# Sigmoid attention and a bilinear layer on one core: bursts of three with the first product group in whole feature blocks, high parts by ScalarE from the 14th burst, later decoding, the first load of k in two pieces

## The chip, the cores and the metric

The kernel runs on one core of a Trainium2 chip. The metric is device microseconds of one execution; the time before is the median of three runs. Engines are called TensorE (PE in the rows, PEld for its weight loads), VectorE (DVE), ScalarE (ACT), GpSimd (POOL) and SyncE (SP), which only issues transfers here.

## The reference

```python
# q, k, v: (8, 12, 448, 64); tokens 8 * 448 = 3584, d_model 768, d_ff 1024
scores = scale * np.matmul(q, k.transpose(0, 1, 3, 2)) - np.log(S)
attn = 1.0 / (1.0 + np.exp(-scores))
x = np.matmul(attn, v)            # heads side by side: (3584, 768)
a, b = x @ w1, x @ w2             # 768 x 1024 each
h = a * b @ w3                    # 1024 x 1024
out = h @ w_out                   # 1024 x 768
```

The weights come as 64-bit floats, and the kernel decodes them on the chip.

## The kernel before, in words

**Attention.** 96 pairs of batch and head make 48 pairs of heads; two of those pairs form a quad `t`, and a quad has seven items: three chunks of 128 keys for the first pair, one short item that holds the last 64 keys of both pairs, and three chunks for the second pair. 24 quads give 168 items in one list. `sizes` cuts the list into bursts. A burst `k` does, in the order of the program: `prepare` of its items (transfers of later q, k and v; at item (0, 1) and (1, 0) the split of the pair that comes next into a high and a low part, where `hi_cast` says which engine makes the high part and VectorE subtracts the low part); some units of other work; the scores of its items (six matmuls for an ordinary item, eight for a short one) each followed by ScalarE's sigmoid; then the attends (four matmuls, eight for a short one) of the burst before. Finished attends are copied out by ScalarE (`combine`, L334). The output of a sigmoid has four buffers.

**Banks.** Two pairs of banks (`sp`) hold scores, two `av` banks hold attends, and an upper pair of banks holds either `third`, the scores of the third item of a burst, or `up0` and `up1`, the accumulators of products. `share_upper` switches it, and the first write under the new name waits for the last reader under the old one.

**Products.** The first layer is done in four groups `g` of two batches each, by a scheme with seven products for a feature block of 128 (L533). A group is eight feature blocks of 7 x 3 x 3 = 63 matmuls, 504 in all (`GROUP`). `up(g)` yields them one matmul at a time; `take(filler, n)` puts n of them at a place in the program. The partial sums leave by ScalarE copies (products 0 and 2 of a block) and VectorE additions (the others, L500 and L503). Behind each product `beside` takes units of other work.

**Where the products stand.** The first group is spread over a window of bursts, `WINDOW`. Before, the window is bursts 18 to 45 (numbered from 0), all of two items, and behind every second one stand 36 matmuls of products. The next two groups stand whole behind the bursts in `blocks`, 51 and 57, which also have two items. The last group comes after attention.

**Other work.** `change` holds 21 units (`Units`) that split the operands of the next group. `weights` decodes w1 and w2: for each feature block 12 steps on VectorE (six for each of the two weights, with one magnitude by ScalarE for each, L89) and 11 steps that make the seven operands of the block (`divide`: a cast by ScalarE, L79, and a subtraction by VectorE, L80) and four differences. The steps of a block's operands stand between the decoding steps of the next block. That is 1 + 96 + 88 = 185 steps. Before a product whose operand does not yet exist, the missing steps are forced (`next(weights)`). All engines run the instructions in the order of the program (`manual_schedule`).

**After attention** come the last group of the first layer, the product of w3 and w_out, and the second layer. The change does not touch them.

Of the kernel before, what the change touches and what calls it, by code (L numbers as in the profile page):

```python
# [11 lines left out]
F32 = mybir.dt.float32  # L12
# [13 lines left out]
def sigmoid_attention_bilinear_ffn(  # L26
# [16 lines left out]
    nc = tc.nc  # L43
    B, H, D, S = qT.shape
    DM, DF = w1.shape[0], w1.shape[1] // 2
    NT = B * S
    P = 128
# [76 lines left out]
    pa = phase_a.enter_context(tc.tile_pool(name="pa", bufs=2, side="right"))  # L124
# [11 lines left out]
    def load_pair(n, queues=(nc.sync, nc.sync)):  # L136
        b, hp = divmod(n, NPAIR)
        heads = slice(2 * hp, 2 * hp + 2)
        qk = pa.tile([P, 2, S], F32, name="qk", bufs=4)
        for i, src in enumerate((qT, kT)):  # L140
            queues[i].dma_start(out=qk[:, i], in_=src[b, heads].rearrange("h d s -> (h d) s"))
        return qk

    def load_v(t, queue=nc.sync):
# [44 lines left out]
    def scores(high, low, c, third, qk):  # L189

        at = c * P
        sp = score_banks(third)
        terms = ((high, high), (high, low), (low, high)) if high else ((qk, qk),)
        for m, (k, q) in enumerate(terms):
            for j, rows in enumerate(HEADS):
                nc.tensor.matmul(  # L196
                    sp[:, j], k[rows, 1, at:at + P], q[rows, 0],
                    start=m == 0, stop=m == len(terms) - 1,
                )
        return sp  # L200

    def short_scores(two, third):

        sp = score_banks(third)
        for u, qk in enumerate(two):
            for j, rows in enumerate(HEADS):
                nc.tensor.matmul(  # L207
                    sp[HEADS[u], j], qk[rows, 1, FULL:], qk[rows, 0], start=True, stop=True
                )
        return sp  # L210

    def attention(sp):
        a = pa.tile([P, 2, S], F32, name="a", bufs=4)
        sigmoid(a, sp)
        return a
# [18 lines left out]
    KH = NK // 2  # L234
# [111 lines left out]
    def prepare_weights():  # L346

        raw = {}

        def load(j):  # L350
            if j < 2 * NF:
                fc, i = divmod(j, 2)
                raw[j] = load_words(
                    words((w1, w2)[i], slice(fc * P, (fc + 1) * P)), p1, nc.gpsimd, 3
                )

        extras = iter(())
        for j in range(3):
            load(j)
        yield  # L360
        nxt = magnitude(raw[0], p1, 3)
        for fc in range(NF):
            fs = []
            for i in range(2):
                f = nxt
                j = 2 * fc + i
                fs.append(f)
                pops = POPS[i] if fc else (0,) * 6
                for step, _ in enumerate(decode(raw[j], f)):
                    if step == 4 and j + 1 < 2 * NF:  # L370
                        nxt = magnitude(raw[j + 1], p1, 3)
                    if step == 5:
                        del raw[j]
                        load(j + 3)
                    yield
                    for _ in range(pops[step]):
                        yield from one(extras)
            extras = finish_weights(fc, fs)
        for _ in range(sum(sum(pops) for pops in POPS)):
            yield from one(extras)  # L380
# [62 lines left out]
    for ic in range(NF):  # L443
# [3 lines left out]
        for ms in (slice(0, NM), slice(NM, DM)):  # L447
            src = w_out[ic * P:(ic + 1) * P].rearrange("p (m u) -> p m u", u=2)[:, ms]
            jobs.append((src, wo_dram[ic, :, ms]))
    def prepare_rest():  # L450

        raw = {}

        def load(i):
            if i < len(jobs):
                raw[i] = load_words(jobs[i][0], p2[0], nc.sync, 4)

        for i in range(3):
            load(i)
        for _ in range(6):  # L460
            yield
        f = magnitude(raw[0], p2[0], 3)
        for i, (_, dst) in enumerate(jobs):
            load(i + 3)
            for step, _ in enumerate(decode(raw.pop(i), f)):
                if step == 4 and i + 1 < len(jobs):
                    following = magnitude(raw[i + 1], p2[0], 3)
                yield
            nc.gpsimd.dma_start(out=dst, in_=f)
            f = following  # L470
# [96 lines left out]
    def take(stream, n):  # L567
        done = 0
        for _ in itertools.islice(stream, n):
            done += 1  # L570
        return done
# [20 lines left out]
    assert len(quad) == TILES  # L592
    items = [(t, x) for t in range(B * NQ) for x in quad]
    GROUP = NF * 7 * KH * 3
    sizes = [3] * 18 + [2] * 28 + [3] * 5 + [2] + [3] * 5 + [2] + [3] * 8
    WINDOW = (18, 46)
    blocks = {51: 1, 57: 2}
    NBURST = len(sizes)
    starts = [sum(sizes[:k]) for k in range(NBURST + 1)]
    bursts = [items[i:i + n] for i, n in zip(starts, sizes)] + [[]]  # L600
# [3 lines left out]
    def beside(g, n):  # L604

        if g == 0:
            take(change, 1)
            take(weights, 2)
        elif not take(change, 1):
            take(rest, 2)  # L610

    qks, splits, vvs = {}, {}, {}
    qks[0] = load_pair(0, (nc.sync, nc.scalar))
    qks[1] = load_pair(1)
    vvs[0] = load_v(0)
    ready = pm.tile([P, 1], F32, name="ready")
# [2 lines left out]
    weights = prepare_weights()  # L619
    for n in (2, 3):  # L620
        qks[n] = load_pair(n)
    filler = rest = iter(())
    change = Units(0)
# [40 lines left out]
    def short_at(burst, at):  # L664

        shorts = [item for item in burst if item[1] is None]
        rest_of = [item for item in burst if item[1] is not None]
        if len(burst) == 3 and burst[1][1] is None:
            return shorts + rest_of if at == 0 else rest_of + shorts
        return list(burst)  # L670

    def prepare(t, x, hi_cast):

        if x == (0, 1):
            splits[2 * t + 1] = split_pair(qks[2 * t + 1], hi_cast)
        elif x == (0, 2) and t + 1 < B * NQ:
            vvs[t + 1] = load_v(t + 1)
        elif x == (1, 0) and t + 1 < B * NQ:
            splits[2 * t + 2] = split_pair(qks[2 * t + 2], hi_cast)
        elif x == (1, 1) and t + 2 < B * NQ:  # L680
            for n in (2 * t + 4, 2 * t + 5):
                qks[n] = load_pair(n)

    for k in range(NBURST + 1):
        if k == WINDOW[1]:
            phase_1.close()
            px.append(phase_x.enter_context(tc.tile_pool(name="px", bufs=1, side="left")))
            p2.append(phase_2.enter_context(tc.tile_pool(name="p2", bufs=2, side="right")))
            rest = prepare_rest()
        in_window = WINDOW[0] <= k < WINDOW[1]  # L690
        hi_cast = nc.scalar.copy if in_window or k in blocks else nc.vector.tensor_copy
        burst = bursts[k]
        for t, x in burst:
            prepare(t, x, hi_cast)
        if k < WINDOW[0]:
            if k == 1:
                next(weights)
            elif k > 1:
                take(change, 3)
                take(weights, 3 if k < 9 else 2 if k < 13 else 1)  # L700
        elif not in_window and k not in blocks and k < NBURST:
            take(change, 4 if k < 51 else 3)
        now = []
        for i, (t, x) in enumerate(short_at(burst, -1)):
            if x is None:
                sp = short_scores((qks.pop(2 * t), qks.pop(2 * t + 1)), i == 2)
            else:
                u, c = x
                if (k, i) == (0, 0):
                    high = low = None  # L710
                else:
                    high, low = splits[2 * t + u]
                sp = scores(high, low, c, i == 2, qks.get(2 * t + u))
            now.append((t, x, attention(sp)))
        if k == NBURST:
            take(change, 4)
            filler = up(NG - 1)
            take(filler, 9)
        by_place = {item[:2]: item for item in now}
        for item in previous:  # L720
            attend_item(*item)
        previous = [by_place[item] for item in short_at(burst, 0)]
        if k == WINDOW[0]:
            filler = up(0)
        if in_window:
            take(weights, 3 if k > WINDOW[0] + 1 else 0)
            done = k + 1 - WINDOW[0]
            if done % 2 == 0:
                upto, since = (GROUP * i // (WINDOW[1] - WINDOW[0]) for i in (done, done - 2))
                take(filler, upto - since)  # L730
            if k + 1 == WINDOW[1]:
                take(filler, 10)
                change = Units(1)
                take(weights, 10 ** 6)
                for n in range(RING - 1):
                    load_weights(NF * 7 + n)
        elif k in blocks:
            filler = up(blocks[k])
            take(filler, GROUP + 10)
            change = Units(blocks[k] + 1)  # L740
# [280 lines left out]
```

## Time and profile before

| what | us |
|---|---|
| median of three runs | 966.53 (966.41 to 967.92) |
| the profiled execution | 964.66 |
| its span in the profile | 962.9 |
| TensorE busy | 955.6 |
| VectorE busy | 657.1 |
| ScalarE busy | 400.2 |

The span runs from the first to the last instruction of the profiled execution; its time adds what lies around them. Busy times of matmuls are modelled, since matmuls overlap; what one costs is best read as the distance from its start to the next one's. The granted TensorE clock is 1.00, the upper of its two levels, 2.4 GHz, in every stretch of the profile.

### The profile page before, as it was taken

What the parts mean: (1) busy time and instruction counts of PE and PEld (TensorE: products, weight loads), DVE (VectorE), ACT (ScalarE), POOL (GpSimd) and SP (SyncE); (2) the same over time, 40 slices, a digit from 0 to 9 for tenths busy, and PEclk for the clock granted to TensorE, in tenths of its full rate; (3) what the DMA queues carried; (4) which work ended last, traced back from release to release, by engine and by line L of the source; (5) the groups of instructions that cost most, each with busy time, mean ns of one, the idle gap of its engine ahead of it and who ended that gap; (6) DMA issues with size and microseconds to landing.
All of it is one profiled execution on the core that took longest, in us unless ns stands there. A gap on an engine that the chain in (4) does not pass through costs nothing.

```text
span 962.9 us, 14120 instructions
## 1 busy us (share of the span) xinstructions
PE 955.6 (99%) x5236; PEld 756.4 (79%) x5236; DVE 657.1 (68%) x1060; ACT 400.2 (42%) x583; POOL 104.8 (11%) x182
## 2 busy tenths in 40 slices
PE   9999999999999999999999999999999999999998
PEld 5444666676674999957999747999999999999997
DVE  5869778887639788899888628444465657474752
ACT  7887456556548121263221474112243523232230
POOL 1110123222200012110111100211000000000000
PEclk9999999999999999999999999999999999999999
DMA  8864577776645899975999734988431033343402
GB/s 268 254 214 132 190 258 240 244 259 233 234 130 171 293 380 379 381 274 173 366 375 355 240 93 131 355 295 285 165 141 62 29 127 123 115 144 111 157 30 86
DMA packets 93781, 204.37 MB, mean 212 GB/s; under 512 B 9872, under 2 KB 57104, under 8 KB 93712
## 3 DMA queue, kind: packets, MB, share of 16 engines
q1 hardware_dynamic: 78432, 142.40, 44.0%
q0 software_dynamic: 15136, 60.83, 17.6%
q8 instruction: 42, 0.69, 0.3%
q10 hardware_dynamic: 144, 0.23, 0.1%
q14 instruction: 27, 0.22, 0.1%
HBM read 148.37 MB, written 55.05 MB: 211 GB/s over the span
## 4 chain that ended last, share of the span: by engine, by line
PE 95%; DVE 2%; DMA 1%; ACT 1%; issue 1%; SPq 0%; DVEq 0%; ACTq 0%
PE up L533 42%; PE av L220 11%; PE sp L196 8%; PE av L985 7%; PE sp L985 7%; PE up L985 7%; PE av L853 3%; PE sp L853 3%; PE av L228 2%; PE third L196 1%; PE sp L207 1%; DMA vv<-vL 1%; PE third L207 1%; ACT a L177 0%; DVE low L80 0%
## 5 line engine op out<-in xcount | busy, mean ns | idle before, releaser
L533 PE MATMUL up<-hS,w 128*128 128x448 f32 x702 | 214.6, 366 | 0.0
L533 PE MATMUL up<-hA,w 128*128 128x448 f32 x510 | 159.5, 367 | 0.3 <-ACT a L177 0.3
L177 ACT ACTIVATE a<-sp,bias 128x896 f32<-128x896 f32 x132 | 129.9, 1010 | 49.8 <-PE sp L196 24.6
L533 PEld LDWEIGHTS up<-hS,w 128*128 128x128 f32 x702 | 131.8, 188 | 14.7 <-issue 3.5
L533 PE MATMUL up<-lS,w 128*128 128x448 f32 x351 | 128.2, 365 | 0.0
L220 PE MATMUL av<-a,vv 128*64 128x448 f32 x576 | 122.8, 551 | 0.1
L533 PEld LDWEIGHTS up<-hA,w 128*128 128x128 f32 x510 | 95.8, 188 | 13.3 <-issue 4.5
L533 PE MATMUL up<-lA,w 128*128 128x448 f32 x255 | 93.2, 365 | 0.0
L220 PEld LDWEIGHTS av<-a,vv 128*64 128x64 f32 x576 | 35.5, 136 | 67.8 <-issue 67.3
L500 DVE TENSOR_TENSOR u<-up,p 128x448 f32<-128x448 f32 x64 | 39.9, 623 | 55.4 <-PE up L533 52.2
L542 ACT COPY p<-up 128x448 f32<-128x448 f32 x31 | 16.6, 534 | 146.8 <-PE up L533 141.5
L533 PEld LDWEIGHTS up<-lS,w 128*128 128x128 f32 x351 | 65.9, 188 | 5.2
L985 PE MATMUL av<-gh,wo 128*128 128x448 f32 x224 | 68.6, 367 | 0.0
L985 PE MATMUL sp<-gh,wo 128*128 128x448 f32 x224 | 68.6, 367 | 0.0
L985 PE MATMUL up<-gh,wo 128*128 128x448 f32 x224 | 68.5, 367 | 0.0
L500 DVE TENSOR_TENSOR u<-up,u 128x448 f32<-128x448 f32 x64 | 39.8, 622 | 32.4 <-PE up L533 31.8
L79 ACT CAST gh<-gf 128x896 fp32r<-128x896 f32 x40 | 35.7, 944 | 56.2 <-PE sp L985 50.0
L80 DVE TENSOR_TENSOR gl<-gf,gh 128x896 fp32r<-128x896 f32 x40 | 41.9, 1087 | 22.7 <-ACT gh L79 22.7
L80 DVE TENSOR_TENSOR low<-qk,high 128x896 fp32r<-128x896 f32 x47 | 51.3, 1091 | 7.4 <-ACT high L79 6.3
L89 ACT ACTIVATE f<-raw 128x768 f32<-128x768 f32 (+2 forms) x48 | 34.5, 718 | 50.5 <-DMA w_dram<-f 17.0
L196 PEld LDWEIGHTS sp<-high 64*128 64x128 f32 x232 | 21.9, 185 | 42.8 <-ACT a L177 31.0
L548 ACT COPY c<-up 128x448 f32<-128x448 f32 x31 | 16.6, 534 | 85.7 <-PE up L533 60.0
(145 smaller groups left out, 1778.3 us busy)
## 6 DMA issues: line engine op xcount, KB each, us to landing
w<-w_dram SPq DMA_DIRECT2D x168, 384.0 KB, 5.9
gf<-g_dram SPq DMA_DIRECT2D x16, 896.0 KB, 5.7
w_dram<-w POOLq DMA_DIRECT2D x36, 384.0 KB, 4.7
raw<-w POOLq DMA_DIRECT2D x16, 768.0 KB, 6.2
qk<-qT SPq DMA_DIRECT2D x48, 224.0 KB, 4.8
qk<-kT SPq DMA_DIRECT2D x47, 224.0 KB, 4.9
out<-o_sb SPq DMA_DIRECT2D x47, 224.0 KB, 2.0
vv<-vL SPq DMA_DIRECT2D x24, 384.0 KB, 3.5
```

The source lines that it names most:

```text
L79: hi_engine(out=dst_hi, in_=src)
L80: lo_engine.tensor_tensor(out=dst_lo, in0=src, in1=dst_hi, op=ALU.subtract)
L89: nc.scalar.activation(f, raw[..., 1].bitcast(F32), AF.Abs, scale=HW_SCALE)
L177: nc.scalar.activation(dst, src, AF.Sigmoid, bias=bias[:n], scale=scale)
L196: nc.tensor.matmul(sp[:, j], k[rows, 1, at:at + P], q[rows, 0], start=m == 0, stop=m == len(terms) - 1,)
L207: nc.tensor.matmul(sp[HEADS[u], j], qk[rows, 1, FULL:], qk[rows, 0], start=True, stop=True)
L220: nc.tensor.matmul(acc[cols, :S], vv[:, c, at:at + D], a[:, j], start=start, stop=stop,)
L228: nc.tensor.matmul(acc[cols, :S], vs[HEADS[u], cols], a[HEADS[u], j], start=ends[u][0], stop=ends[u][1],)
L500: nc.vector.tensor_tensor(out=out, in0=a, in1=b, op=ALU.add)
L533: nc.tensor.matmul(a, w[:, i, kc], x, start=bool(start) and kc == 0 and m == 0, stop=bool(stop) and kc == KH - 1 and m == 2, skip_group_ch ...
L853: nc.tensor.matmul(acc, a[:, jc], w[:, jc, ms], start=(jc == 0 and m == 0), stop=(jc == NF - 1 and m == 2),)
L985: nc.tensor.matmul(acc, w[:, fc, ms], g[:, fc], start=start and fc == 0 and m == 0, stop=fc == NH - 1 and m == 2, skip_group_check=True,)
```

## The change

The bursts all have three items. The window becomes bursts 18 to 36, and the first group stands there in whole feature blocks of 63 matmuls behind bursts 19, 22, 24, 27, 29, 32, 34 and 36. The two whole groups stand behind bursts 42 and 48, of three items as well. ScalarE makes the high parts from burst 13 to the end of the window, before from burst 18. Decoding steps: three per burst up to burst 10 (before: to 8), two in 11 and 12, none from 13 to 19 (before: one per burst from 13 to 17), four per burst in the window from burst 20 (before: three), two behind a product of the first group, one behind the last two of each block (before: always two). The first pair's k is loaded in two pieces on ScalarE's queue, the first 128 columns first; q stays on SP's.

```diff
+    def load_first_pair():
+        qk = pa.tile([P, 2, S], F32, name="qk", bufs=4)
+        q, k = (src[0, :2].rearrange("h d s -> (h d) s") for src in (qT, kT))
+        nc.scalar.dma_start(out=qk[:, 1, :P], in_=k[:, :P])
+        nc.sync.dma_start(out=qk[:, 0], in_=q)
+        nc.scalar.dma_start(out=qk[:, 1, P:], in_=k[:, P:])
         return qk
...
-    sizes = [3] * 18 + [2] * 28 + [3] * 5 + [2] + [3] * 5 + [2] + [3] * 8
-    WINDOW = (18, 46)
-    blocks = {51: 1, 57: 2}
+    sizes = [3] * 56
+    WINDOW = (18, 37)
+    FIRST_BLOCKS = [WINDOW[0] + i - 1 for i in itertools.accumulate((2, 3, 2, 3, 2, 3, 2, 2))]
+    blocks = {42: 1, 48: 2}
...
         if g == 0:
             take(change, 1)
-            take(weights, 2)
+            take(weights, 2 if n % 7 < 5 else 1)
...
-    qks[0] = load_pair(0, (nc.sync, nc.scalar))
+    qks[0] = load_first_pair()
...
-        hi_cast = nc.scalar.copy if in_window or k in blocks else nc.vector.tensor_copy
+        hi_cast = nc.scalar.copy if 13 <= k < WINDOW[1] or k in blocks else nc.vector.tensor_copy
...
-                take(weights, 3 if k < 9 else 2 if k < 13 else 1)
+                take(weights, 3 if k < 11 else 2 if k < 13 else 0)
         elif not in_window and k not in blocks and k < NBURST:
-            take(change, 4 if k < 51 else 3)
+            take(change, 4 if k < 42 else 3)
...
         if in_window:
-            take(weights, 3 if k > WINDOW[0] + 1 else 0)
-            done = k + 1 - WINDOW[0]
-            if done % 2 == 0:
-                upto, since = (GROUP * i // (WINDOW[1] - WINDOW[0]) for i in (done, done - 2))
-                take(filler, upto - since)
+            take(weights, 4 if k > WINDOW[0] + 1 else 0)
+            if k in FIRST_BLOCKS:
+                take(filler, 7 * KH * 3)
```

## Rows read from the trace of the kernel before

**Rows 1.** From the page: the busy time of each engine with its share of the span and its instructions, and the chain of waits that ended last, by engine.

```profile
PE 955.6 (99%) x5236; PEld 756.4 (79%) x5236; DVE 657.1 (68%) x1060; ACT 400.2 (42%) x583; POOL 104.8 (11%) x182
...
PE 95%; DVE 2%; DMA 1%; ACT 1%; issue 1%; SPq 0%; DVEq 0%; ACTq 0%
```

**Rows 2.** Timeline of TensorE, the early stretch with bursts of three: the first scores of a burst, and those seven bursts later. Columns: start in us, length in us, engine, line, operation, output and inputs, count, in brackets the idle time before it and what ended it.

```profile
45.55 0.47 PE L196 MATMUL sp<-high 64*128 64x448 f32 x2
...
77.98 0.47 PE L196 MATMUL sp<-high 64*128 64x448 f32 x2
```

**Rows 3.** The same view in the window, bursts of two: the start of attention behind products and the start of the next products, three times, then the start of attention and of the eighth burst.

```profile
230.72 0.61 PE L207 MATMUL sp<-qk 64*64 64x448 f32 x4
...
237.32 0.47 PE L533 MATMUL up<-hA,wo 128*128 128x448 f32 x1
...
244.83 0.47 PE L196 MATMUL sp<-high 64*128 64x448 f32 x2
...
251.28 0.47 PE L533 MATMUL up<-hA,w 128*128 128x448 f32 x1
...
258.82 0.47 PE L196 MATMUL sp<-high 64*128 64x448 f32 x2
...
265.12 0.47 PE L533 MATMUL up<-hS,wo 128*128 128x448 f32 x1
...
272.62 0.47 PE L196 MATMUL sp<-high 64*128 64x448 f32 x2
...
275.70 0.61 PE L207 MATMUL sp<-qk 64*64 64x448 f32 x4
```

**Rows 4.** The chain of waits in order of time, a segment of products in the window and the whole second group: start in us, length in us, what.

```profile
167.17 7.50 PE up L533 x36
...
313.08 102.39 PE up L533 x504
```

**Rows 5.** Timeline of TensorE in bursts 15 and 16: two waits.

```profile
79.58 0.47 PE L196 MATMUL sp<-low,high 64*128 64x448 f32 x2 [0.52 <-DVE low L80]
...
84.84 0.47 PE L196 MATMUL sp<-low,high 64*128 64x448 f32 x2 [0.39 <-DVE low L80]
```

**Rows 6.** Groups of instructions with shapes kept apart: busy us, mean ns of one, idle time before them. The high part by VectorE and by ScalarE, the magnitude of a weight, and the cast of an operand.

```profile
L79 DVE CAST high<-qk 128x896 fp32r<-128x896 f32 x31 | 19.3, 622 | 19.8 <-PE sp L196 12.8 <-DMA qk<-kT 6.9
...
L79 ACT CAST high<-qk 128x896 fp32r<-128x896 f32 x16 | 15.1, 947 | 0.0
L89 ACT ACTIVATE f<-raw 128x768 f32<-128x768 f32 x16 | 14.8, 926 | 9.7 <-DVE w L80 7.2 <-DVE wo L80 2.6
...
L79 ACT CAST w<-f 128x384 fp32r<-128x384 f32 x25 | 12.6, 518 | 5.1 <-PE up L533 3.7 <-DVE f L246 1.3
```

**Rows 7.** Busy us of the engines in two stretches (the early bursts, mid window): stretch, its length, busy time with count for PE, PEld, DVE, ACT and POOL, granted clock, share of the DMA engines, GB/s.

```profile
45.50:54.90 9.40, 9.40 (x69) 4.34 (x67) 7.29 (x11) 7.77 (x11) 0.97 (x2) 1.00 0.36 114
150.00:200.00 50.00, 50.00 (x284) 34.24 (x285) 44.28 (x73) 31.02 (x47) 13.63 (x22) 1.00 0.75 248
```

**Rows 8.** Timeline of TensorE: the first scores of burst 18 and of burst 46.

```profile
88.76 0.47 PE L196 MATMUL sp<-high 64*128 64x448 f32 x2
...
286.70 0.47 PE L196 MATMUL sp<-high 64*128 64x448 f32 x2
```

**Rows 9.** Timeline: a product that waits for an evacuation, a magnitude that waits for VectorE and the scores behind it, and the weight load of the first third item behind the second group.

```profile
114.23 0.47 PE L533 MATMUL up<-hS,wo 128*128 128x448 f32 x1 [0.26 <-DVE c L500]
...
133.04 0.95 ACT L89 ACTIVATE f<-raw 128x768 f32<-128x768 f32 x1 [1.30 <-DVE wo L80]
...
135.78 0.47 PE L196 MATMUL sp<-high 64*128 64x448 f32 x2 [0.53 <-ACT a L177]
...
416.90 0.15 PEld L207 LDWEIGHTS third<-qk 64*64 64x64 f32 x4 [0.38 <-DVE u L500]
```

**Rows 10.** Timeline of two bursts of three: the sigmoid of the third item on ScalarE, and the start of the next burst on TensorE, which is where the attends end; in the second burst also the sigmoid before.

```profile
68.17 1.00 ACT L177 ACTIVATE a<-third,bias 128x896 f32<-128x896 f32 x1
68.81 0.47 PE L196 MATMUL sp<-high 64*128 64x448 f32 x2
...
427.68 1.01 ACT L177 ACTIVATE a<-sp,bias 128x896 f32<-128x896 f32 x1 [0.71 <-PE av L220]
428.59 1.00 ACT L177 ACTIVATE a<-third,bias 128x896 f32<-128x896 f32 x1
429.01 0.61 PE L207 MATMUL sp<-qk 64*64 64x448 f32 x4
```

**Rows 11.** The end of attention: the last attends and the first product of the last group in TensorE's timeline, and between them the sigmoids in the chain of waits.

```profile
580.24 0.98 PE L228 MATMUL av<-a,vs 64*64 64x448 f32 x8
581.56 0.47 PE L533 MATMUL up<-hA,w 128*128 128x448 f32 x1 [0.34 <-ACT a L177]
...
579.60 1.91 ACT a L177 x2
```

**Rows 12.** Timeline of the start: q and k are there (the first casts of their high parts), the first scores, and the weight load of the first attend.

```profile
4.18 0.56 ACT L167 CAST high<-qk 128x448 fp32r<-128x448 f32 x1 [1.51 <-DMA qk<-qT]
4.36 0.39 DVE L168 CAST high<-qk 128x448 fp32r<-128x448 f32 x1 [2.93 <-DMA qk<-kT]
...
4.38 1.86 PE L196 MATMUL sp<-qk 64*128 64x448 f32 x4
...
10.66 0.20 PEld L220 LDWEIGHTS av<-a,vv 128*64 128x64 f32 x4 [0.51 <-DMA vv<-vL]
```

More of the change, by code (lines that the diff above doesn't have):

```diff
@@ L141, in load_pair @@
             queues[i].dma_start(out=qk[:, i], in_=src[b, heads].rearrange("h d s -> (h d) s"))
+        return qk
+    def load_first_pair():
[4 more added lines that the diff above has]
+        nc.scalar.dma_start(out=qk[:, 1, P:], in_=k[:, P:])
         return qk
```

## The prediction

> **What bounds the kernel now.** I read the busy times first, then the chain of waits, then stretches of the timeline. TensorE is busy 955.6 of 962.9 us and the chain that ends last is 95% TensorE [rows 1], so any change in the time must be a change in what TensorE does or waits for. The run that was profiled took 964.66 us, 1.8 us more than its span and 1.9 us (0.2%) less than the median of 966.53; I work out a difference on the profiled run and add it to the median. All edits lie in the stretch up to the end of attention, so the reader should look at the price of a burst, of a start of products, and at the waits between them. Below 0.2% (1.93 us) a difference cannot be told from none here. Bursts are numbered from 0, as in the code; the 14th is burst 13.
>
> **Fewer bursts (gain).** With bursts of three in the early stretch, seven bursts (21 items) take from 45.55 to 77.98 us, 32.43 us, 4.633 us each [rows 2]. With bursts of two in the window, the four stretches of attention between product segments are 6.60, 6.45, 6.30 and, to the start of the last burst, 3.08 us: seven bursts (14 items) in 22.43 us, 3.204 us each [rows 3]. Both cycles hold the same mix of six regular items and one short one. So an item costs 4.633 - 3.204 = 1.429 us and a burst by itself 3.204 - 2 x 1.429 = 0.346 us (TensorE changes from scores to attend and back). The list of sizes has 18 + 28 + 20 = 66 bursts before and 56 after, for the same 168 items: 10 x 0.346 = **3.5 us less**. Bound from the other side: nothing, if third items in the window are held up; that I price as waits below.
>
> **Fewer starts of products (gain).** A segment of 36 matmuls takes 7.50 us, a block of 504 takes 102.39 [rows 4]: (102.39 - 7.50) / 468 = 0.2028 us per matmul, and 7.50 - 36 x 0.2028 = 0.20 us for the start. The first group goes from 14 segments to 8 blocks of 63: 6 x 0.20 = **1.2 us less**.
>
> **High parts by ScalarE from the 14th burst, decoding later (gain).** In the 16th and 17th burst TensorE waits 0.52 and 0.39 us for VectorE's low part [rows 5]. VectorE is behind there because the operands of the first group and the decoding share it. A cast of the high part costs VectorE 0.622 us [rows 6]; taking it away in bursts 13 to 17 (about 0.86 per burst) together with one decoding step per burst (0.56 to 0.96 us) frees 1.1 to 1.5 us per burst, some 3 us by the 16th burst, more than the two waits. I take both as gone: **0.9 us less**; the bound is nothing. The two steps that are added earlier, in bursts 9 and 10, fall where VectorE is busy 7.29 of 9.40 us [rows 7]; the 2.1 us left cover them, and if that cover failed the price would be the same sort of wait, up to 0.5 us. On ScalarE the cast costs 0.947 us [rows 6], 0.81 us per burst. It is busy 7.77 of 9.40 us in the early stretch [rows 7] and loses the decoding's share from burst 13 on, so it has no time left over but is not over full.
>
> **Waits in the window of the first group (some gain).** From the scores of the 19th burst to those of the 47th 197.94 us pass [rows 8]. 28 bursts at 3.204, 14 segments at 7.50 and 0.8 us for a third item attended at the start make 195.5, so 2.4 us are waits: for example 0.53 us for ScalarE behind a decoding magnitude that itself had waited 1.30 us for VectorE, and 0.26 us for an evacuation by VectorE [rows 9]. The change removes none of this work. Per block it now paces 12 steps, and 4 per burst, against 14 steps per two bursts and 36 matmuls: over 2.375 bursts and a block (about 24 us) 21.5 steps instead of 24.5 in the same time, so VectorE, busy 44.28 of 50 us in mid window [rows 7], gets some 5% relief. What is late next is the evacuation at the end of a block: the third item of the next burst needs both product banks back. In the block of the second group this is already at its edge (TensorE held up 0.38 us at its weight load [rows 9]). In the new blocks the last two products have 0.62 + 0.63 us of evacuation and one step for 1.83 us of TensorE, so VectorE comes out level or a little late; I take 0.2 us per block, 1.6 us, against the 2.4 us of before: **0.8 us less**. Bounds: 2.4 us less if all is clean, 2 us more if each block loses what the old stretch lost in two.
>
> **Third item right before a block (loss).** The bank pair of the third scores and the product banks are one memory. Before, segments in the window and the two long blocks follow a burst of two, which uses no third bank. Now all ten blocks follow a burst with a third item, and the first product must wait for its sigmoid. In an ordinary burst of three that sigmoid starts 0.91 us behind the second, which waited for the first attend to free its output (0.71 us idle), and ends at 429.59, while TensorE has finished the attends at 429.01; in the next sample 69.17 against 68.81 [rows 10]. With 0.05 us to get going, that would be a wait of 0.63 and 0.41 us. At the end of attention the wait stands in the trace itself: the last attends start at 580.24 and take 0.98, the third sigmoid ends at 581.51, and products start at 581.56 [rows 11], some 0.35 us after the attends. Over bursts of three like these I see 0.41 to 0.67. Ten blocks: 4.1 to 6.7 us; the rows between give about 0.56 each, **5.6 us more**. The other bound adds ScalarE's queue: the steps of the burst before stand ahead of the sigmoids. Counting through the cycle of 23 steps per feature block, before the blocks at bursts 22, 24 and 27 come two casts (0.52 us each), or a magnitude (0.93) and two casts, and the high part's 0.95 [rows 6]; with overlaps that moves the third sigmoid by 0.4, 1.2 and 1.2 us, 8.4 us in all. I take 5.6 because ScalarE, with the decoding's casts among its work, was busy 83% in the early stretch [rows 7] and its third sigmoids there still end 0.41 to 0.67 us late: the second sigmoid waits for the attend anyway.
>
> The row shows ScalarE idle for 0.71 us ahead of the second sigmoid while the queue holds later work [rows 10]. The Trainium skill, TensorE: Matmul & The Clock Gate, section "Architectural detail: the array is 16x 32x32, not 1x 128x128", says ScalarE and VectorE are strict FIFO; the trace agrees, and this speaks against giving ScalarE more to do ahead of sigmoids: by it, with every cast ahead counted in full, the sum below would end 2.8 us higher.
>
> **First load of k in two pieces (nothing).** q and k land within 0.2 us of each other and the first scores start at 4.38. But the first attend starts at 10.66, held by the load of v [rows 12], which stands on SP behind the same transfers as before; ScalarE's queue gets one more issue of 0.4 us during which it waits for q anyway. What hides the edit is v's load; without it the gain would be the 0.2 us by which k is later than q, and if the second piece lands later the loss is of that size. I take 0.
>
> **Sum.** -3.5 - 1.2 - 0.9 - 0.8 + 5.6 = -0.8 us: 965.7 us, within 0.2%.
>
> **The rivals.**
> *Faster: blocks and bursts run clean.* VectorE's relief removes all 2.4 us and the ten waits come out at the low end, 0.45: -3.5 - 1.2 - 0.9 - 2.4 + 4.5 = -3.5, **963.0 us**. For it: VectorE idles more in the new pacing and no step is forced. Against it: most rows give 0.5 to 0.65. If the wait for the third sigmoid did not exist at all, -8: 958.5; the row at 581.56 speaks against that.
> *Slower: ScalarE's order in the window.* Per attention burst ScalarE has three sigmoids at a pitch of 0.91 us, 0.86 casts, 0.86 copies and about 0.2 us per step: 2.73 + 0.74 + 0.38 + 0.81 = 4.66 us with overlaps taken off, against 4.63 for TensorE. It decides once ScalarE is so late that the first sigmoid of a burst ends after TensorE wants its bank, some 2.4 us of lag. Then every following sigmoid is late too: ten waits at 8.4 us and 0.15 us in each of the 19 bursts of the window (2.9 us): -3.5 - 1.2 - 0.9 - 0.8 + 8.4 + 2.9 = +4.9, **971.4 us**. For it: the 0.53 us wait of rows 9 is this one. Against it: each block gives ScalarE some 6 us to catch up.
> *Slower: operands too late.* Steps offered fall from 225 to 196 where 185 are needed. If products have to force steps, each costs a cast and a subtract, 1.1 us; one per block is 8.8 us, +8, **974.5 us**. Against it: by count each operand is made two products ahead.
> That the edits do nothing at all is excluded: the bursts and blocks are in the program's order.
>
> **Chances.** Forecast, within about 1.9 us of 966.5: 0.43. Clean run: 0.36. ScalarE's order: 0.16; operands: 0.05. So faster 0.36, same 0.43, slower 0.21. The range leaves out a tenth at each end: below, the clean run with 0.3 us of scatter, 962.7; above, half of ScalarE's price, 969.2. The likeliest case's own range is 964.6 to 968.0.
>
> **What would show it.** Right: each of the ten blocks starts 0.4 to 0.7 us after the attends, 0.05 us behind a third sigmoid; bursts in the window take 4.6 us; the two waits of the 16th and 17th burst are gone; attention ends (first product of the last group) within 2 us of 581.6. Wrong: starts of blocks more than 1 us late, third scores waiting for an evacuation after blocks, or product streams with gaps in front of a weight load for decoded operands.

## The result and the profile after

The changed kernel takes 974.66 us (median of six runs, 971.78 to 976.68) against 965.96 us for the kernel before (six runs): a ratio of 1.0092, 95% interval 1.0077 to 1.0107. The forecast was 965.7 us in a range up to 969.2; the change makes the kernel 0.9% slower. The profiled run took 975.75 us with a span of 973.9 us, 11.0 us longer than the one of before.

TensorE did the same work in about the same busy time, but fell from 99% to 98% of the span, and ScalarE came into the chain of waits, with 4% where it had 1% [rows 1]. From the page of the changed kernel:

```profile
PE 954.5 (98%) x5236; PEld 762.5 (78%) x5236; DVE 654.0 (67%) x1053; ACT 404.9 (42%) x590; POOL 104.7 (11%) x182
...
PE 88%; ACT 4%; issue 4%; DMA 1%; POOL 1%; DVE 1%; SPq 0%; DVEq 0%; ACTq 0%; POOLq 0%
```

The timeline of TensorE shows where: the first product of each of the ten blocks (start, length, engine, line, operation, tiles, count, idle time before and what ended it). In the kernel before the only such wait was the 0.34 us of [rows 11].

```profile
99.09 0.47 PE L541 MATMUL up<-hA,w 128*128 128x448 f32 x1 [0.56 <-ACT a L185]
...
127.80 0.47 PE L541 MATMUL up<-hA,wo 128*128 128x448 f32 x1 [1.51 <-ACT a L185]
...
152.22 0.57 PE L541 MATMUL up<-hA,w 128*128 128x448 f32 x1 [2.02 <-ACT a L185]
...
183.27 0.74 PE L541 MATMUL up<-hA,w 128*128 128x448 f32 x1 [2.45 <-ACT a L185]
...
209.00 0.47 PE L541 MATMUL up<-hA,wo 128*128 128x448 f32 x1 [1.99 <-ACT a L185]
...
238.63 0.47 PE L541 MATMUL up<-hA,w 128*128 128x448 f32 x1 [1.08 <-ACT a L185]
...
261.45 0.47 PE L541 MATMUL up<-hA,w 128*128 128x448 f32 x1 [0.40 <-ACT a L185]
...
285.38 0.47 PE L541 MATMUL up<-hA,wo 128*128 128x448 f32 x1 [0.56 <-ACT a L185]
...
326.69 0.47 PE L541 MATMUL up<-hA,w 128*128 128x448 f32 x1 [0.56 <-ACT a L185]
...
457.49 0.47 PE L541 MATMUL up<-hA,w 128*128 128x448 f32 x1 [0.40 <-ACT a L185]
```

The ten waits are 11.5 us by these rows (12.2 us from start to start, since a matmul's modelled end lies 0.07 us behind the next one's start). Five are the 0.40 to 0.56 us of an ordinary third sigmoid; five, behind bursts 22 to 32, are 1.1 to 2.5 us. The chain of waits in front of the third block says why they are long (start, length, what):

```profile
146.68 0.57 DVE wo L80
147.25 0.02 issue
147.27 0.05 ACT f L89
147.32 0.80 issue
148.12 0.50 ACT wo L79
148.62 0.84 ACT high L79
149.46 2.72 ACT a L185 x3
152.17 0.04 issue
152.22 3.86 PE up L541 x10
```

VectorE finishes an operand's low part; only then can ScalarE start the next magnitude (0.85 us), and behind it stand the cast of another operand, the cast of a high part, and then the three sigmoids of the burst. TensorE waits for the last of them. The ten products at the end of the chain take 3.86 us, 0.39 us each instead of 0.20: the clock had fallen. The same length, 3.4 us, from the start of four blocks (stretch, its length, busy time with count for PE, PEld, DVE, ACT and POOL, granted clock, DMA share, GB/s):

```profile
127.80:131.20 3.40, 3.40 (x17) 3.15 (x18) 2.95 (x6) 1.79 (x4) 0.56 (x1) 1.00 0.86 300
152.20:155.60 3.40, 3.38 (x10) 2.99 (x11) 2.54 (x5) 1.21 (x3) 1.22 (x2) 0.54 0.96 271
183.25:186.65 3.40, 3.38 (x9) 3.04 (x10) 2.95 (x6) 1.21 (x3) 1.31 (x2) 0.51 0.27 110
210.00:213.40 3.40, 3.40 (x12) 3.02 (x11) 2.93 (x5) 1.49 (x4) 1.39 (x2) 0.57 0.50 187
```

Seventeen matmuls run in the first of these stretches and nine to twelve in the others, at a granted clock near 0.5, which is the lower level, 1.2 GHz. Three blocks of 63 (behind bursts 24, 27 and 29) take 14.5 to 14.6 us instead of 13.0, 4.7 us together.

Two smaller losses: in bursts 9 and 10 TensorE loses 1.4 us behind a magnitude that waited for VectorE, and in the block at 261 us a product waits for its operand; that block takes 14.1 us.

```profile
49.56 0.96 ACT L89 ACTIVATE f<-raw 128x768 f32<-128x768 f32 x1 [2.60 <-DVE w L80]
51.47 0.47 PE L204 MATMUL sp<-high 64*128 64x448 f32 x2 [0.87 <-ACT a L185]
...
264.23 0.47 PE L541 MATMUL up<-hS,w 128*128 128x448 f32 x1 [0.68 <-ACT w L79]
```

What the prediction counted as gains is there. Bursts in the window, from the first scores of one to those of the next, take 4.59 and 4.56 us, like the 4.633 of [rows 2], and the two waits of [rows 5] do not return:

```profile
112.07 0.47 PE L204 MATMUL sp<-high 64*128 64x448 f32 x2
...
116.66 0.47 PE L204 MATMUL sp<-high 64*128 64x448 f32 x2
...
121.22 0.59 PE L215 MATMUL sp<-qk 64*64 64x448 f32 x2
```

The parts can be added up over the stretch from the first scores of burst 18 to the first product of the last group:

```profile
89.12 0.47 PE L204 MATMUL sp<-high 64*128 64x448 f32 x2
...
592.67 0.47 PE L541 MATMUL up<-hA,w 128*128 128x448 f32 x1 [0.34 <-ACT a L185]
```

It takes 503.55 us, before 492.80 ([rows 8] and [rows 11]): 10.75 us more. The ten waits (12.2), the low clock (4.7) and the product that waits for its operand (1.1) make 18.0 us, so some 7.3 us were gained. Ahead of burst 18 the loss of 1.4 us in bursts 9 and 10 takes back what the two waits of [rows 5] gave.

### The profile page after: what moved, and what is told of

It is laid out like the page before. It is cut to its first block, busy times and chain, and to the rows that moved or that the text cites. A ratio compares the mean times of both kernels' runs of the same rounds, so it can differ in the third digit from the quotient of the medians.

```text
span 973.9 us, 14151 instructions
## 1 busy us (share of the span) xinstructions
PE 954.5 (98%) x5236; PEld 762.5 (78%) x5236; DVE 654.0 (67%) x1053; ACT 404.9 (42%) x590; POOL 104.7 (11%) x182
## 4 chain that ended last, share of the span: by engine, by line
PE 88%; ACT 4%; issue 4%; DMA 1%; POOL 1%; DVE 1%; SPq 0%; DVEq 0%; ACTq 0%; POOLq 0%
PE up L541 40%; PE av L228 9%; PE av L992 7%; PE sp L992 7%; PE up L992 7%; PE sp L204 6%; PE sp L860 3%; PE av L860 3%; ACT a L185 3%; PE third L204 2%; PE av L236 2%; PE third L215 1%; DMA vv<-vL 1%; POOL w_dram L416 1%; DMA g_dram<-c 0%
## 5 line engine op out<-in xcount | busy, mean ns | idle before, releaser
L541 PE MATMUL up<-hA,w 128*128 128x448 f32 x510 | 162.0, 372 | 7.8 <-ACT a L185 7.8
L185 ACT ACTIVATE a<-sp,bias 128x896 f32<-128x896 f32 x112 | 112.0, 1012 | 78.5 <-PE sp L204 42.4
L228 PE MATMUL av<-a,vv 128*64 128x448 f32 x576 | 120.6, 549 | 0.5 <-DMA vv<-vL 0.5
L185 ACT ACTIVATE a<-third,bias 128x896 f32<-128x896 f32 x56 | 56.3, 1005 | 0.0
L541 PEld LDWEIGHTS up<-lA,w 128*128 128x128 f32 x255 | 48.7, 191 | 3.7
```

Of the source, the lines that this page charges most:

```text
L185: nc.scalar.activation(dst, src, AF.Sigmoid, bias=bias[:n], scale=scale)
L228: nc.tensor.matmul(acc[cols, :S], vv[:, c, at:at + D], a[:, j], start=start, stop=stop,)
L541: nc.tensor.matmul(a, w[:, i, kc], x, start=bool(start) and kc == 0 and m == 0, stop=bool(stop) and kc == KH - 1 and m == 2, skip_group_ch ...
```

## The experiments

Theory A: the first product of a block waits for the third sigmoid because third scores and products use the same banks; the wait is long because ScalarE runs its queue in order and the window's casts and magnitudes stand ahead of the sigmoids; the clock falls in these long waits. Rivals: ScalarE has too much work in the window whatever the banks (B); the clock falls for another reason (C); VectorE is late and ScalarE only waits for it (D).

### No third item ahead of a block

```diff
-    sizes = [3] * 56
+    sizes = [2 if k in FIRST_BLOCKS or k in blocks or k > 57 else 3 for k in range(60)]
```

> The changed kernel, but the ten bursts ahead of a block of products (and the last two) have two items, so no third scores stand in the product banks: 60 bursts instead of 56. In the changed kernel the ten blocks start 12.3 us late in sum, and three of them run their first 3.4 us at half the TensorE clock, which costs another 4.7 us. Theory A (the first product waits for the third sigmoid, which ScalarE's in-order queue makes late, and the falls of the clock follow from the long waits): both go, four bursts more cost 4 x 0.35 = 1.4 us: 974.7 - 12.3 - 4.7 + 1.4 = 959 us. Rival B (ScalarE simply has too much work in the window, whatever the bank): the lateness moves into the scores of the next bursts, and at least half of the 17 us stays: 966 us or more. Rival C (the clock falls for another reason than the waits): the three slow stretches stay, 964 us.

Measured: 964.75 us, ratio to before 0.9988 (0.9977 to 1.0000). The ten waits are gone: the shared banks are the place of the wait. In the profiled run the granted clock is 1.00 throughout, so the three falls went with the waits, against C. But three of the ten runs, the slowest, have a mean clock of 0.998, as the profiles with one fall have, so a fall can still come. And 10 us came back, not 16. Inside the blocks products now wait 4.5 us in sum, where the changed kernel had about 1.2, for example behind the first evacuation and behind an operand's cast (timeline of TensorE):

```profile
149.86 0.47 PE L541 MATMUL up<-hS,wo 128*128 128x448 f32 x1 [0.56 <-DVE u L508]
...
220.29 0.47 PE L541 MATMUL up<-hS,wo 128*128 128x448 f32 x1 [0.41 <-ACT wo L79]
```

So B holds in part, with the lateness in products and not in scores. Another 1.8 us of the profiled run lie in the last group of products, which the edit does not touch (see the load of k below).

### Less for ScalarE: casts of operands, or high parts, by VectorE

```diff
-            split(w[:, 0], w[:, 1], src, nc.scalar.copy, nc.vector)
+            split(w[:, 0], w[:, 1], src, nc.vector.tensor_copy, nc.vector)
```

> The changed kernel, but VectorE makes the high part of the decoded operands (56 casts of 128x384, 0.52 us each on ScalarE, about 0.36 us on VectorE). Theory A: one or two casts fewer stand ahead of each late sigmoid, and the magnitude no longer waits behind them; the waits ahead of blocks fall from 12.3 to about 8 us and the falls of the clock go: 966 us. Rival D (VectorE is what is late, ScalarE only waits for it): VectorE gets 20 us more work in the window, waits and slow stretches grow: 977 us or more.

Measured: 967.53 us, ratio 1.0020 (1.0005 to 1.0035), 7 us faster than the changed kernel, with no fall of the clock in the profiled run; four of the eight runs have a mean clock of 0.998. The waits are 7.7 us in sum, as A expected. Nine shrink to the 0.4 to 0.6 us of an ordinary third sigmoid. One stays long, and again a magnitude is ahead of it that waited for VectorE (timeline of TensorE and ScalarE):

```profile
126.89 0.47 PE L541 MATMUL up<-hA,wo 128*128 128x448 f32 x1 [0.56 <-ACT a L185]
149.87 0.47 PE L541 MATMUL up<-hA,w 128*128 128x448 f32 x1 [0.56 <-ACT a L185]
...
174.81 0.95 ACT L89 ACTIVATE f<-raw 128x768 f32<-128x768 f32 x1 [1.55 <-DVE w L80]
...
179.34 0.47 PE L541 MATMUL up<-hA,w 128*128 128x448 f32 x1 [2.43 <-ACT a L185]
```

```diff
-        hi_cast = nc.scalar.copy if 13 <= k < WINDOW[1] or k in blocks else nc.vector.tensor_copy
+        hi_cast = nc.scalar.copy if 13 <= k < 18 or k in blocks else nc.vector.tensor_copy
```

> The changed kernel, but VectorE makes the high parts in the window again (bursts 18 to 36; ScalarE keeps bursts 13 to 17). Theory A: 0.95 us less ahead of the sigmoids of seven of the eight block bursts: waits from 12.3 to about 6.5 us, no falls of the clock: 964 us. Rival D (VectorE late): 10 us more work for VectorE, no gain or a loss: 975 us or more.

Measured: 968.91 us, ratio 1.0021 (1.0008 to 1.0035); the ten waits come to 8.8 us from start to start instead of 12.2, where A expected 6.5 us and a time of 964 us, and none of the blocks runs at the low clock. Both edits put work on VectorE, and both help: D, as the main cause, is out. In this profile, of the slowest of nine runs, the clock fell once elsewhere, in the early loss, which was longer here (timeline of TensorE, then busy times of the stretch with the granted clock before the last two columns):

```profile
51.54 0.47 PE L204 MATMUL sp<-high 64*128 64x448 f32 x2 [1.98 <-ACT a L185]
```

```profile
51.90:55.30 3.40, 3.37 (x20) 1.28 (x16) 2.81 (x4) 3.40 (x6) 0.29 (x1) 0.57 0.02 5
```

### The idle time and the clock

```diff
             if k in FIRST_BLOCKS:
+                if k in (24, 27, 32):
+                    idle = ps.tile([P, 2, 512], F32, name="sp", bufs=2)[:, 0, :S]
+                    for _ in range(8):
+                        nc.tensor.matmul(idle, splits[max(splits)][0][:, 0, :P],
+                                         splits[max(splits)][0][:, 0], start=True, stop=True)
                 take(filler, 7 * KH * 3)
```

Eight matmuls stand behind the attends of three bursts. The edit was meant for the three blocks that ran at the low clock; the third of these stands behind burst 29, not 32, so the edit and its expectation miss that one.

> The changed kernel with eight matmuls of no use, into a score bank that is free, between the attends and the blocks behind bursts 24, 27 and 32, where TensorE waits 2.0 to 2.5 us for the third sigmoid; they fit into the wait (8 x 0.2 us). If the falls of the clock come from TensorE standing idle there: no fall, the three blocks take 13.0 instead of 14.5 us, 4.7 us less, 970 us. If they come from something else in these stretches (or from a slow start of the products): falls and time stay, 974.7 us.

Measured: three runs, 971.19, 975.56 and 975.82 us. The first was profiled, and its clock is 1.00 through all stretches of the window: the two blocks with the matmuls ahead take 13.0 us instead of 14.5, the block behind burst 29 starts after a wait as long as before (1.98 us) and runs at the upper level too, and the run is 4.6 us faster than the profiled run of the changed kernel. The stretches in which these three blocks start:

```profile
150.00:154.00 4.00, 3.96 (x19) 3.44 (x20) 2.42 (x5) 3.02 (x5) 0.99 (x2) 1.00 0.98 332
179.50:183.50 4.00, 4.00 (x19) 3.48 (x20) 2.47 (x5) 3.01 (x6) 0.95 (x2) 1.00 0.54 209
205.50:209.50 4.00, 3.94 (x19) 3.67 (x20) 2.78 (x5) 2.54 (x6) 1.33 (x2) 1.00 0.61 239
```

The other two runs have a mean clock of 0.998 and are no faster than the changed kernel. So where the idle time was filled the clock did not fall, as A has it, but this is one run, in which it did not fall behind the long wait that was left either. That it is the idle time that brings the clock down is therefore made likely, not shown. By the median the edit gives nothing. What the other two runs lost stays open; the clock is not enough, since the changed kernel took 971.78 us in its run at 0.998.

### Decoding in the early stretch, and the load of k

```diff
-                take(weights, 3 if k < 11 else 2 if k < 13 else 0)
+                take(weights, 3 if k < 9 else 2 if k < 13 else 0)
```

> The changed kernel with the decoding pace of before in bursts 9 and 10 (two steps instead of three). The changed kernel loses 1.4 us in bursts 8 and 9 (48.9 to 52.3 us), where a magnitude on ScalarE waits 2.60 us for VectorE ahead of the sigmoids. If the third step causes it: the loss goes, 973.3 us, and the waits at the blocks stay about what they are. If it has another cause (transfers of the start): it stays.

Measured in two runs: 973.57 us, ratio 1.0080 (1.0053 to 1.0107). The loss, which lies in bursts 9 and 10, is gone, so the third step caused it. The time is close to the 973.3 us expected, but its interval holds the changed kernel's ratio too. The waits ahead of the blocks did not stay what they were (10.1 us in sum, the longest now 3.18), and with two steps fewer in hand a later block waits longer for an operand. In the timeline of TensorE:

```profile
258.88 0.47 PE L541 MATMUL up<-hS,w 128*128 128x448 f32 x1 [1.87 <-ACT w L79]
```

```diff
-    qks[0] = load_first_pair()
+    qks[0] = load_pair(0, (nc.sync, nc.scalar))
```

> The changed kernel, but the first k in one load as before. In the changed kernel the first attend starts at 10.98 us instead of 10.66. If the split is the cause (the second piece comes later, and so does everything behind it on the transfer engines): the first attend is back at 10.66 and the time 0.3 us lower. If the later v is chance: no difference at the first attend.

Measured: 973.50 us, ratio 1.0071 (1.0048 to 1.0093), and the first attend starts at 10.96 us against 10.98, held by v in both (the changed kernel, then the single load).

```profile
10.98 0.60 PE L228 MATMUL av<-a,vv 128*64 128x448 f32 x2 [0.51 <-DMA vv<-vL]
```

```profile
10.96 1.35 PE L228 MATMUL av<-a,vv 128*64 128x448 f32 x6 [0.91 <-DMA vv<-vL]
```

The split does nothing that can be seen; over all runs here the first attend starts anywhere from 9.9 to 11.1 us.

The profile of the single load shows a loss that is not in the waits and not in the granted clock: its third group of products takes 2.0 us longer than that of the changed kernel. From start to start a matmul takes 0.2067 us instead of 0.2027, all through the group (busy times of the stretch, the changed kernel first):

```profile
457.49:559.83 102.34, 102.34 (x505) 94.64 (x506) 80.57 (x157) 18.05 (x34) 15.97 (x30) 1.00 0.94 329
```

```profile
456.04:560.38 104.34, 104.34 (x504) 94.51 (x504) 80.47 (x157) 18.12 (x34) 16.19 (x30) 1.00 0.93 323
```

In other profiles most matmuls of a long group are as slow: of the last group with no third item, with high parts by VectorE, with the early pace and with the moved steps below, and of the second group with operand casts by VectorE on the kernel before. The kernel before and the changed kernel, as profiled, have it in no long group. Its cause stays open, and a difference of 2 us between two profiled runs can be this alone.

### The mends together, and steps in hand

Two items ahead of the blocks, operand casts by VectorE, the early pace of the last section and the single load:

> Two items ahead of each block, operand casts by VectorE, the early pace and the single load of k together. Theory A with its mends adding up: 964.75 (two items) less 1.4 us (early pace) less some 3 us of the 4.5 us that the blocks there still lose (operands late on ScalarE at 220 and 242 us): 960 us. If VectorE is the next bound (it gets 20 us of casts, and the waits for its evacuation at 150 and 177 us grow): 965 us or more.

Measured: 962.18 us, ratio 0.9968 (0.9950 to 0.9987): faster than both kernels, and between the two outcomes. What remains lost in the window is products that wait, now for VectorE: 0.85 us for an evacuation at 174 us, and for an operand:

```profile
192.80 0.47 PE L541 MATMUL up<-hS,w 128*128 128x448 f32 x1 [1.05 <-DVE w L79]
```

With operand casts left on ScalarE, and the steps moved away from the bursts right ahead of blocks (in the window's bursts 64 are offered instead of 68):

```diff
-            take(weights, 4 if k > WINDOW[0] + 1 else 0)
+            take(weights, 0 if k < WINDOW[0] + 2 else 2 if k in FIRST_BLOCKS else 5)
```

> Two items ahead of each block, the early pace, the single load, operand casts by ScalarE as in the changed kernel, but two decoding steps instead of four in the bursts right ahead of blocks and five in the others. If the evacuations late at 150 and 177 us come from the steps that stand ahead of the block on VectorE: those 2.5 us go as well as the 1.4 us of the early pace, 961 us. If operands get late instead: waits for the casts of operands in the blocks grow, 965 us.

Measured: 972.40 us, ratio 1.0068 (1.0043 to 1.0093). The worse outcome, and worse than priced: products wait up to 3 us for the cast of their operand.

```profile
245.51 0.47 PE L541 MATMUL up<-hS,w 128*128 128x448 f32 x1 [2.99 <-ACT w L79]
```

Then the version with all mends, with more steps in hand:

```diff
-                take(weights, 3 if k < 9 else 2 if k < 13 else 0)
+                take(weights, 3 if k < 9 else 2 if k < 13 else 1)
```

> The version with all mends (two items ahead of blocks, operand casts by VectorE, single load of k), but with the decoding pace of the kernel before in the whole early stretch, one step per burst from 13 to 17 too: five steps more in hand. If its remaining losses (products that wait 1.2 and 1.4 us at 174 and 193 us) come from operands and evacuations that are late because decoding is paced too tightly: 2 us less, 960 us. If the early steps bring back the waits for the low parts in bursts 15 and 16: no gain or a loss, 963 us.

Measured: 960.18 us, ratio 0.9944 (0.9929 to 0.9958), the best version of this study. The two waits are smaller (0.71 us below, and 0.15), and the early steps bring back one wait for a low part, smaller than the two of [rows 5]:

```profile
88.91 0.47 PE L204 MATMUL third<-low,high 64*128 64x448 f32 x2 [0.25 <-DVE low L80]
...
174.34 0.47 PE L541 MATMUL up<-hS,w 128*128 128x448 f32 x1 [0.71 <-DVE u L508]
```

### Single parts on the kernel before

The operand casts by VectorE alone, the same edit as above:

> The kernel before with one edit, the casts of decoded operands by VectorE. If the gain of the version with all mends is the gain of that edit alone: 962.5 us. If the edit only cures what the bursts of three brought, and the kernel before has little of it (2.4 us of waits in the window): within 1.5 us of before, either way.

Measured: 969.97 us, ratio 1.0044 (1.0029 to 1.0059): slower by more than either expectation. The edit that gains 7 us in the changed kernel loses 4 here. In mid window VectorE is busy 47.41 of 50 us, against 44.28 [rows 7], and low parts and evacuations come later than before (busy times by stretch, and the timeline of TensorE):

```profile
150.00:200.00 50.00, 49.52 (x280) 33.14 (x279) 47.41 (x83) 25.38 (x33) 13.32 (x22) 1.00 0.71 234
```

```profile
85.36 0.47 PE L196 MATMUL sp<-low,high 64*128 64x448 f32 x2 [0.57 <-DVE low L80]
...
202.95 0.47 PE L533 MATMUL up<-hS,w 128*128 128x448 f32 x1 [0.81 <-DVE u L500]
```

In the profiled run 3.1 us are lost up to burst 46; another 2.0 us lie in the second group, with the slower matmuls told above. The gain of the mended version is therefore not that edit's alone. That it needs the bursts of three follows only by elimination: no run has all other mends with bursts of two.

The early part alone:

```diff
-        hi_cast = nc.scalar.copy if in_window or k in blocks else nc.vector.tensor_copy
+        hi_cast = nc.scalar.copy if 13 <= k < WINDOW[1] or k in blocks else nc.vector.tensor_copy
...
-                take(weights, 3 if k < 9 else 2 if k < 13 else 1)
+                take(weights, 3 if k < 9 else 2 if k < 13 else 0)
```

> The kernel before with the early part of the change alone: high parts by ScalarE from burst 13, no decoding steps in bursts 13 to 17. By the prediction: the two waits for VectorE's low parts (0.52 and 0.39 us) go, 0.9 us less. Against it: five steps fewer in hand make operands late in the window, and the sum is a loss of 1 us or more.

Measured: 965.49 us, ratio 1.0000 (0.9991 to 1.0010). The two waits of [rows 5] go, as predicted, but by the median nothing is gained. In the profiled run, the slowest of ten, TensorE waits in the window instead, not for operands but behind sigmoids that are late, since a magnitude ahead of them had waited for VectorE (timelines of ScalarE and TensorE). Behind this wait the clock falls (busy times of the stretch, the granted clock before the last two columns):

```profile
160.10 0.95 ACT L89 ACTIVATE f<-raw 128x768 f32<-128x768 f32 x1 [1.95 <-DVE w L80]
...
162.83 0.47 PE L196 MATMUL sp<-high 64*128 64x448 f32 x2 [1.34 <-ACT a L177]
```

```profile
164.50:168.00 3.50, 3.50 (x11) 1.10 (x10) 3.22 (x6) 3.03 (x6) 1.39 (x2) 0.53 0.29 112
```

Whole blocks alone, with the bursts of two kept:

```diff
-            done = k + 1 - WINDOW[0]
-            if done % 2 == 0:
-                upto, since = (GROUP * i // (WINDOW[1] - WINDOW[0]) for i in (done, done - 2))
-                take(filler, upto - since)
+            if (k + 1 - WINDOW[0]) % 7 in (0, 3):
+                take(filler, 7 * KH * 3)
```

> The kernel before, bursts of two kept, with the first group in eight whole blocks of 63 matmuls (behind bursts 20, 24, 27, 31, 34, 38, 41 and 45) instead of 14 segments. By the prediction's term: six starts fewer, 1.2 us less, and no wait for a third sigmoid, 964.5 us. If whole blocks by themselves make operands or evacuations late: 967 us or more.

Measured: 964.82 us, ratio 0.9993 (0.9984 to 1.0002). The median is 0.8 us less, where the term had 1.2, but the interval does not tell it from nothing.

## Why the prediction was wrong, point by point

**Fewer bursts, fewer starts: right as far as they can be told apart.** Bursts of three in the window cost what the early ones did. The 7.3 us gained behind burst 18 are about the two terms (3.5 and 1.2 us) and the 2.4 us of waits in the old window. No run has fewer bursts alone, and whole blocks alone cannot be told from nothing.

**Third item right before a block: the place right, the size wrong.** This is the step that failed. The prediction took 5.6 us and named 8.4 as its other bound; the rows show 11.5. Its own sign of being wrong, blocks that start more than 1 us late, came at five of the ten. The sentence that failed is the reason for the choice: that the second sigmoid waits for the attend anyway, so that work ahead of the sigmoids hides. That is so for five blocks. Where two casts and a high part stand ahead, or a magnitude or cast that has itself waited for VectorE, the queue is later than the attend, and the wait is 1.1 to 2.5 us. The count through the cycle of steps had named three of these five (22, 24 and 27) with 2.8 us above the ordinary wait; the rows show 4.3 there, and 2.0 more behind bursts 29 and 32, which it left out. Behind 29 a cast waited 1.75 us for VectorE, which had waited for ScalarE's copy of an attend; behind 32 a magnitude waited 0.63 us for VectorE, which had waited for ScalarE's earlier cast. The count by steps assumed a queue that never waits. The in-order queue of ScalarE, weighed and set aside there, was the better guide; moving the casts to the other engine gave back 7 us, although VectorE has the higher busy share of the window, in the kernel before 44.28 of 50 us against 31.02 [rows 7].

**The clock: missing altogether.** No term and no rival asked what a wait of 2 us does to TensorE behind it. In the profiled run that is 4.7 us of the 11, and the changed kernel's six runs are ordered by it: 971.78 us at a mean clock of 0.998, 975.75 and 976.68 at 0.995. It is not the whole spread: the version with the single load took 976.65 us at 0.996, with the slow third group. In the kernel before, the clock is 1.00 through all of its stretches, so no row there could price it.

**High parts and decoding early: right at its place, nothing in sum.** The two waits went. They lie in bursts 16 and 17 counted from 0, one later than [rows 5] and the prediction say, and cost 1.4 us from burst to burst, more than the 0.9 us of idle time that the prediction took. The early part alone gains nothing in sum. That the five steps not made there are missing later is not shown by it; in the version with all mends five more steps gave 2 us. And the two steps added in bursts 9 and 10, costed at nothing because VectorE had 2.1 us free, lost 1.4 us, where the prediction had 0.5 at most: the cover was a share over a stretch, but the magnitude waited 2.60 us for one instruction of VectorE and then stood ahead of the sigmoids.

**Window: the waits for evacuations behind blocks did not come; the operands did.** The term of 0.8 us was too small, since it kept 1.6 us for those evacuations. The prediction gave 0.05 to the case that operands are late. In the changed kernel it is one product (0.68 us), but each of the two versions with operand casts by ScalarE and fewer steps, the early pace and the moved steps, met more of it, up to 3 us per product. That this rival's 974.5 us lies next to the measured 974.66 is luck.

**The load of k: right.** v hides it.

**The slower rival** (ScalarE's order, 971.4 us) names the mechanism that decided, at 0.16; it had put 2.9 us into the bursts, where nothing was lost, and only 2.8 us more into the blocks, where the rows show 5.9 more.

## What to carry to other kernels

When two uses share a bank, price the switch by the whole queue of the engine that must release it: list what stands ahead of the releasing instruction, and what each of those waits for in turn, not their durations alone. A share of busy time does not say that a step is covered; the queue of the engine that has to release the waiting one does. And moving work from one engine to another is worth what the waiting engine stood behind: the same edit gave 7 us in one of these kernels and cost 4 in the other.

## What the runs showed of the hardware

TensorE's clock fell to its lower level nine times in the profiled runs, each time at a wait of TensorE: from 0.1 us before its end to 1.9 us behind it. In the changed kernel the waits were 2.02, 2.45 and 1.99 us, in the other versions 2.01, 2.48, 1.98, 1.87, 3.18 and, in the early part alone, 1.34 us. The length does not decide alone: eleven other waits of 1.49 to 2.99 us were followed by no fall, among them 2.43 us with operand casts on VectorE and the 2.99 us of the moved steps. A fall cost about 1.6 us in a stretch that is bound by matmuls. The profiles with one fall have a mean clock of 0.998, those with two 0.996, and the one with three 0.995.

At a granted clock of 1.00 a matmul of the long groups took 0.2027 us in most profiles and 0.2067 us, for a whole group or most of one, in others.
